# Part B of a two-part attention kernel: two projection passes split around other blocks, and the sums of the output rows moved into the next segment

## The chip, the cores and the metric

One core of a Trainium2 chip runs the whole program. The metric is the device time of one execution in microseconds (us). The engines are TensorE (PE, with its weight loads PEld), VectorE (DVE), ScalarE (ACT), GpSimd (POOL), and SyncE (SP), which here only issues DMAs.

## What is computed

The program has two parts, with their outputs side by side. Part A, a local dilated attention over 2048 rows, is not touched. Part B is a recurrence over 64 segments of 32 rows. Each segment puts 8 memory rows ahead of its 32 rows, attends over all 40 with 32 heads of 192, and the first 8 rows of its result are the memory of the next segment:

```
mem = mem0
for s in range(n_seg):                               # 64
    h = concatenate([mem, x[32*s : 32*s + 32]])      # 40 x 640
    q, k, v = h @ Wq, h @ Wk, h @ Wv                 # 32 heads x 192
    p = softmax(mask(q @ k.T * scale))
    o = (p @ v) @ Wo                                 # 40 x 640
    mem = o[:8];  outs.append(o[8:])
```

## The kernel before

**The split of the rows.** Of the 40 rows of a segment, 32 depend on the memory of the segment or stand right behind it: 8 memory rows and 24 rows of the input. They are `HX[:, 0]`, called `main`. The last 8 rows of a segment depend on no memory, so they can be projected segments ahead: `HX[:, 1]`, called `ahead`, holds them for four segments. What is projected from `ahead` is called late: the kernel keeps late queries and keys in buffers (`Lb`) and late values in the value tiles (`Vg`), and writes late output rows at the very end.

**Groups.** The 32 heads make 4 groups of 8. A segment takes the groups in the order 0, 1, 2, 3 when s is even and 3, 2, 1, 0 when s is odd. In a name such as `k.2` the number is the place in that order, not the group. Per group there are these steps, each a function of `part_b`:

- `q`, `k`, `v`: projection passes on PE (L554), 20 matmuls of 32 x 384 for `main`, five pieces (`dc`) of 4 matmuls. Where the group is renewed (`RENEW`, L295), `ahead` is projected in the same pass: 40 matmuls. One key group is renewed per segment: at s mod 4 = 0 or 3 it is the first one (`k.0`), at 1 or 2 the third (`k.2`).
- `e`: ACT (one of four by DVE) copies the projection out of PSUM (L560 for the late part, L593); `T`: DVE turns it 32 x 32 in place (L564), POOL copies the late columns (L579, L584, L600).
- `S`: 16 score matmuls (L623); `sb`, `mx`, `sub`, `send`: the softmax on DVE (L629 to L655) with the exponential on ACT (L641); the result is the tile `P`.
- `tp`: PE turns `P` (L663); `PT`: ACT or DVE spreads it (L670, L673); `mix`: PE multiplies with the values (L685); `ot`: DVE and ACT copy the result to the tile `OT` (L693), POOL copies its late rows to `OL` (L694) and sends them to HBM (L695).
- `out`: 24 matmuls with the output weights into the sum `Y` (L710); the fourth group's are the step `last`.

Between segments stand four more. `ql` projects the late rows for one query group (20 matmuls), `eql` copies them out and `Tql` turns them; DVE does it in the tile `sb`, which has one buffer, and POOL then copies four pieces of it (L584). `vl` projects them for one value group (20 matmuls), `vel` copies that out (ACT, L614, two copies). `close` makes the new memory rows of `Y`: DVE turns two halves (L522) and adds them into `HX` (L721), from where `q.0` of the next segment reads. Then it sums the output rows: ACT copies two halves of `Y` to scratch in `OT` (L725), DVE adds them to the others in `YS` (L727), and four stores of `YS` are put on a list that SP issues at `k.0` of the next segment (L765).

**What sets the order.** PE, DVE, ACT and SP run their instructions in the order in which they are written, and that is the string `ORDER` (L303; `FIRST` for segment 0). POOL's order is found by the tile framework.

**Weights.** Groups 0 and 3 share their slots for q, v and o. When the first group in a segment has been used, SP loads the other one into the slot from a copy in HBM (`change`, L412): query weights behind `q.0`, value weights behind `v.0`, output weights in two pieces behind the two halves of the first `out`. The last output group reads the latter. One fifth of a key group is swapped behind `k.0` (L399). A DMA issue of SP stands behind all earlier ones of SP.

Of the kernel before, what the change touches and what calls it, by code (L numbers as in the profile page):

```python
# [23 lines left out]
def part_a(ctx, tc, A_x, A_wqkv, A_wo, out, ident, emit_loads):  # L24
# [288 lines left out]
SHARED = (0, 3)  # L313
# [11 lines left out]
def part_b(ctx, tc, B_x, B_mem0, B_Wq, B_Wk, B_Wv, B_Wo, out, ident, n_seg, pre, mid):  # L325
    nc = tc.nc
    Dm, H, Dh, M, SEG, L = 640, 32, 192, 8, 32, 40
# [386 lines left out]
    def close(s, Y):  # L714
        if s + 1 < n_seg:
            T = [KT[:].rearrange("p f n -> p (f n)"), QT[:]]
            T = [t[:, 0:320].bitcast(FP32).rearrange("p (k n) -> p k n", n=SEG) for t in T]
            for b in range(2):
                turn32(T[b], Y[:, 160 * b:160 * b + 160])
            for b in range(2):  # L720
                nc.vector.tensor_tensor(HX[64 * b:64 * b + 64, 0, :, 0:M], T[b][0:64, :, 0:M], T[b][64:128, :, 0:M],  # L721
                                        op=ALU.add)
        half = OT[:].rearrange("p c n -> p (c n)")[:, 0:320].bitcast(FP32)
        for b in range(2):
            S_(half[64 * b:64 * b + 64], Y[64:128, 160 * b:160 * b + 160])  # L725
        for b in range(2):
            nc.vector.tensor_tensor(YS[64 * b:64 * b + 64], Y[0:64, 160 * b:160 * b + 160],  # L727
                                    half[64 * b:64 * b + 64], op=ALU.add)
        stores.extend((out2[SEG * s:SEG * s + SEG - M, Dm + 160 * j:Dm + 160 * j + 160], YS[32 * j + M:32 * j + SEG])
                      for j in range(4))  # L730
        if s + 1 == n_seg:
            while stores:
                nc.gpsimd.dma_start(*stores.pop(0))

    stores = []

    def segment(s):
        last = s + 1 == n_seg
        engine = {"S": S_, "V": V_}
        got = {}  # L740
# [10 lines left out]
        def step(name, *at):  # L751
            n = int(at[0][-1]) if at else None
            g = turn[n] if at else None
            if name in "qkv":
                project(name, g)
                if name == "q" and n == 0:
                    change(name, g, slice(0, 2))
                    change(name, g, slice(2, 5))
                    load_x(s + 1)
                if name == "v" and n == 0:  # L760
                    change(name, g)
                if name == "k" and n == 0:
                    replace(*(PAIR if g == PAIR[0][1] else PAIR[::-1]))
                    while stores:
                        nc.sync.dma_start(*stores.pop(0))  # L765
                if s == 0 and n == 0 and name != "q":
                    load_all("o", 1 if name == "k" else 2)
                if last and name == "v" and n == 1:
                    load_outputs()
            elif name == "e":  # L770
                m = at[0][0]
                got["sb", m, g] = evacuate(m, got.pop((m, g)), [engine[c] for c in EVACUATE[at[0]]])
            elif name == "T":
                m = at[0][0]
                keep = fill_late(s, m, g, got.pop(("sb", m, g)))
                turn_in_place(columns_of(m, 0, 32))
                if at[0] == "k0" and s and keep:
                    got["keep"] = keep
                elif keep:
                    keep()  # L780
                if at[0] == "k1" and "keep" in got:
                    got.pop("keep")()
            elif name == "S":
                got["S", g] = scores(g)
            elif name == "sb":
                got["t", g] = soft_begin(got.pop(("S", g)))
            elif name == "mx":
                got["mx", g] = soft_max(got["t", g])
            elif name == "sub":
                soft_exp(got["t", g], got.pop(("mx", g)))  # L790
            elif name == "send":
                soft_end(s, g, got.pop(("t", g)))
            elif name == "tp":
                got["p", g] = turn_p(g)
            elif name == "PT":
                got["PT", g] = spread_p(got.pop(("p", g)), SPREAD[n])
            elif name == "ve":
                keep_values(g, got.pop(("v", g)))
            elif name == "mix":
                got["mix", g] = mix(g, got.pop(("PT", g)))  # L800
            elif name == "ot":
                keep_mix(s, g, got.pop(("mix", g)), [engine[c] for c in HEADS[n]])
            elif name == "out":
                half = int(at[1])
                if "Y" not in got:
                    got["Y"] = ps_y.tile([128, 320], FP32, tag="y", name="Y")
                n = int(at[0])
                g = turn[n]
                project_out(got["Y"], g, range(4 * half, 4 + 2 * half), n == 0, False)
                if n == 0 and not last:  # L810
                    change("o", g, slice(4 * half, 4 + 2 * half))
                if n == 0 and half and last:
                    load_late(range(4))
# [80 lines left out]
    with tc.manual_schedule(engines={mybir.EngineType.PE, mybir.EngineType.DVE, mybir.EngineType.Activation,  # L894
                                     mybir.EngineType.SP}):
        for s in range(n_seg):
            segment(s)
        project_late()


# [67 lines left out]
```

## Time and profile before

| what | value |
|---|---|
| runs | 1717.2, 1717.04, 1709.44 us (median 1717.04) |
| the profiled execution | 1717.32 us |
| its span, first to last instruction | 1715.4 us |
| mean granted TensorE clock | 0.997 |
| busy: PE, PEld, DVE, ACT, POOL | 93%, 59%, 66%, 58%, 31% |
| moved by DMA | 474.80 MB, 277 GB/s in the mean |

A row of the timeline has start and length in us, engine, line, operation, tiles written and read, shape, count of instructions merged, and in brackets the idle time of the engine before it with what ended it. Lengths of matmuls overlap, since they are pipelined: the time that a block takes is the difference between its start and the next block's. A row of the waits has waiting engine and line, what ended the wait, us in total, times, and the longest. DMA issues stand as SPq and their time is that of the issue, not of the transfer.

### The profile page before, as it was taken

To read this page: it belongs to the slowest core of one execution; us is meant where nothing else is said; L and a number is where in the kernel's file an instruction comes from. 1 tells how busy PE (TensorE), PEld (TensorE's weight loads), DVE (VectorE), ACT (ScalarE), POOL (GpSimd) and SP (SyncE) were. 2 spreads that over 40 slices of the span, in tenths; PEclk is the share of its full clock that TensorE was granted. 3 is DMA by queue.
4 is the path that set the end of the run, shared out by engine and by line. 5 is a ranking of instruction groups with operands and counts; after the bars stand their busy time and mean duration, and the time that the engine had idled before them with its cause. 6 is when DMAs were issued, how large, how long until landed. Compare 5 with 4: busy or idle time off the path is not lost.

```text
span 1715.4 us, 82589 instructions
## 1 busy us (share of the span) xinstructions
PE 1596.4 (93%) x35702; PEld 1015.7 (59%) x35702; DVE 1130.4 (66%) x3334; ACT 989.1 (58%) x2544; POOL 536.1 (31%) x1592
## 2 busy tenths in 40 slices
PE   7999899999999999999999999899999999999988
PEld 5666555555555555555565555555555555555668
DVE  4987566667666666766666766666767666666730
ACT  3554556666665666655666665566666655665630
POOL 0201233333333333333333333333333333333320
PEclk9999999999999999999999999999999999999999
DMA  7995877778777778877777887777788777777870
GB/s 215 343 293 216 338 279 272 277 287 305 284 278 272 264 274 304 301 263 272 265 287 289 304 301 262 264 277 277 296 304 302 276 274 277 271 296 286 305 301 18
DMA packets 123816, 474.80 MB, mean 277 GB/s; under 512 B 46884, under 2 KB 61842, under 8 KB 99004
## 3 DMA queue, kind: packets, MB, share of 16 engines
q1 hardware_dynamic: 112940, 458.35, 72.0%
q0 software_dynamic: 9696, 10.30, 1.9%
q8 instruction: 280, 4.59, 1.0%
q10 hardware_dynamic: 816, 0.88, 0.2%
q14 instruction: 84, 0.69, 0.1%
HBM read 455.29 MB, written 26.78 MB: 281 GB/s over the span
## 4 chain that ended last, share of the span: by engine, by line
PE 62%; DVE 14%; DMA 13%; ACT 4%; issue 4%; POOL 3%; SPq 0%; ACTq 0%; DVEq 0%; POOLq 0%
PE acc L554 27%; PE Y L710 11%; DMA wres_o<-wcopy_o 7%; PE px L623 7%; PE pq L102 4%; PE px L685 3%; DVE sb L564 3%; PE px L663 3%; DMA wres_q<-wcopy_q 2%; POOL Lb L584 2%; ACT Vg L614 2%; ACT sb L560 2%; DVE KT L564 2%; PE px L863 2%; PE po L168 1%
## 5 line engine op out<-in xcount | busy, mean ns | idle before, releaser
L554 PEld LDWEIGHTS <-HX 128*32 128x32 bf16 x19380 | 495.9, 97 | 297.0 <-DVE HX L721 43.6
L554 PE MATMUL acc<-wres_q,HX 128*32 128x384 bf16 x6460 | 324.2, 327 | 23.0 <-DVE HX L721 19.9
L554 PE MATMUL acc<-wres_v,HX 128*32 128x384 bf16 x6460 | 325.8, 328 | 7.3 <-issue 6.5
L554 PE MATMUL acc<-wres_k,HX 128*32 128x384 bf16 x6460 | 313.8, 326 | 3.3 <-issue 2.1
L710 PE MATMUL Y<-wres_o,OT 128*32 128x320 bf16 x6120 | 278.1, 301 | 26.5 <-issue 11.6
L608 ACT CAST Vg<-acc 64x384 bf16<-64x384 f32 x512 | 241.4, 471 | 50.2 <-PE acc L554 46.4
L694 POOL COPY OL<-OT 128x96 bf16<-128x96 bf16 x256 | 158.1, 617 | 333.5 <-DMA late_o<-OL 143.9
L710 PEld LDWEIGHTS <-OT 128*32 128x32 bf16 x6144 | 148.7, 96 | 97.6 <-issue 36.3
L593 ACT CAST QT<-acc 128x384 bf16<-128x384 f32 x256 | 122.9, 480 | 102.9 <-PE px L623 96.5
L623 PE MATMUL px<-KT,QT 64*64 64x40 bf16 (+1 forms) x4096 | 138.5, 189 | 27.2 <-DVE KT L564 12.5
L695 POOL DMA_DIRECT2D late_o<-OL x256 | 137.9, 539 | 75.4 <-POOL OL L694 54.6
L600 POOL COPY QT<-Lb 128x96 bf16<-128x96 bf16 x252 | 67.6, 268 | 298.0 <-PE px L623 298.0
L623 PEld LDWEIGHTS <-QT 64*64 64x64 bf16 (+1 forms) x4096 | 107.8, 109 | 87.6 <-issue 36.2
L693 DVE CAST OT<-px 128x240 bf16<-128x240 f32 x192 | 78.2, 407 | 107.4 <-PE acc_mix L685 92.0
L670 ACT ACTIVATE PT<-px,own 128x160 bf16<-128x160 f32 x384 | 130.5, 392 | 27.5 <-PE px L663 21.5
L564 DVE STREAM_TRANSPOSE KT<-KT 128x384 bf16<-128x384 bf16 x256 | 141.5, 553 | 2.6 <-ACT KT L593 2.6
L564 DVE STREAM_TRANSPOSE QT<-QT 128x384 bf16<-128x384 bf16 x256 | 143.2, 559 | 0.0
L584 POOL COPY Lb<-sb 128x96 bf16<-128x96 bf16 x453 | 104.3, 268 | 120.9 <-DVE sb L564 120.9
L629 DVE SCALAR_TENSOR_TENSOR px<-px,mask 128x160 f32<-128x160 f32 x256 | 84.7, 331 | 85.7 <-PE px L623 82.1
L693 ACT CAST OT<-acc_mix 128x240 bf16<-128x240 f32 x256 | 92.2, 360 | 78.8 <-PE acc_mix L685 58.4
L593 ACT CAST KT<-acc 128x384 bf16<-128x384 f32 x256 | 123.2, 481 | 14.7 <-PE acc L554 6.9
L685 PEld LDWEIGHTS <-Vg 128*128 128x128 bf16 (+1 forms) x2048 | 86.5, 104 | 72.9 <-issue 25.4
(103 smaller groups left out, 1977.7 us busy)
## 6 DMA issues: line engine op xcount, KB each, us to landing
wres_v<-wcopy_v SPq DMA_DIRECT2D x64, 1920.0 KB
wres_o<-wcopy_o SPq DMA_DIRECT2D x63, 1280.0 KB
wres_q<-wcopy_q SPq DMA_DIRECT2D x64, 1152.0 KB
wres_q<-wcopy_q SPq DMA_DIRECT2D x64, 768.0 KB
wres_o<-wcopy_o SPq DMA_DIRECT2D x63, 640.0 KB
wres_k<-wcopy_k SPq DMA_DIRECT2D x64, 384.0 KB
wres_k<-in_B_Wk_dram SPq DMA_DIRECT2D x19, 384.0 KB
late_o<-OL POOLq DMA_DIRECT2D x256, 24.0 KB, 4.3
```

Source lines behind the costliest of these rows:

```text
L554: nc.tensor.matmul(ps[n][t:t + 32].rearrange("p (f n) -> p f n", n=32), lhsT=X[:, dc, :], rhs=columns(w, (m, g, dc), j), start=(dc == 0), ...
L564: nc.vector.transpose(t, t)
L584: nc.gpsimd.tensor_copy(late[m, g, t][:], rows(t))
L593: copies[1](columns_of(m, 0, 32), ps[-1][:].rearrange("p (f n) -> p f n", n=32))
L608: S_(VG[g][64 * r:64 * r + 64, r], ps[-1][64 * r:64 * r + 64])
L623: nc.tensor.matmul(Sps[64 * h:64 * h + 64, a, :], lhsT=QT[k0:k1, L * f:L * f + 64], rhs=KT[k0:k1, f, :], start=(outer == 0 and a == 0), st ...
L670: nc.scalar.activation(PT[:, :, b], pt.rearrange("p r (h n) -> p (r h) n", h=2)[:, :, 0:L], ACTF.Copy, scale=own[:, b:b + 1])
L685: nc.tensor.matmul(ps[r][lo:hi, 2 * L * k:2 * L * k + 2 * L], lhsT=VG[g][:, r, col:col + hi - lo], rhs=PT[:, 2 * r + h].rearrange("p b n - ...
L693: copy(OT[:, 6 * r:6 * r + 6].rearrange("p c n -> p (c n)"), ps[r][:, 0:6 * L])
L694: nc.gpsimd.tensor_copy(OL[:, g % 2].rearrange("p n c -> p c n"), OT[:, :, 32:L])
L695: nc.gpsimd.dma_start(late_o[s // 4][:, g, s % 4], OL[:, g % 2].rearrange("p n c -> p (n c)"))
L710: nc.tensor.matmul(Y[t:t + 32].rearrange("p (b c) -> p b c", b=2), lhsT=OT[:, slot(c), 0:32], rhs=quarter(w, u, 2 * r + gv), start=first a ...
```

## The change

Three edits of the order of steps, none of the work.

1. `vl` becomes `vl1` and `vl2`. `vl1` has two of the five pieces (8 matmuls) and stands where `vl` stood, ahead of `last`; `vl2` has the other three (12 matmuls) and stands behind `last`. Both add into the same PSUM tile.
2. The sums of the output rows leave `close` and become the step `ys`, in `keep_rows`. It stands in the next segment behind `T.q0`. The four stores are then issued by SP at that place, behind the issues of `k.0` as before. Behind the last segment `keep_rows` is called on its own, with its stores on POOL as before.
3. `q.2` becomes `qa.2` (two pieces, 8 matmuls) ahead of `S.1` and `qb.2` (three pieces, 12 matmuls) behind it.

```diff
 ORDER = """
-    q.0 e.q0 k.0 T.q0 e.k0 T.k0 q.1 k.1 S.0 sb.0 mx.0 e.q1 T.q1 v.0 e.k1 k.2 sub.0 ve.0 T.k1 S.1 send.0 q.2 v.1
+    q.0 e.q0 k.0 T.q0 ys e.k0 T.k0 q.1 k.1 S.0 sb.0 mx.0 e.q1 T.q1 v.0 e.k1 k.2 sub.0 ve.0 T.k1 qa.2 S.1 send.0 qb.2 v.1
     e.k2 sb.1 tp.0 mx.1 q.3 sub.1 e.q2 T.k2 send.1 PT.0 tp.1 T.q2 mix.0 ve.1 ot.0 S.2 sb.2 e.q3 mx.2 PT.1
     out.0.0 k.3 v.2 out.0.1 mix.1 sub.2 T.q3 e.k3 send.2 ve.2 T.k3 S.3 tp.2 ot.1 out.1.0 sb.3 out.1.1 mx.3 PT.2
-    mix.2 sub.3 v.3 send.3 tp.3 ot.2 tx ve.3 PT.3 out.2.0 out.2.1 mix.3 vl ot.3 last ql close vel eql Tql
+    mix.2 sub.3 v.3 send.3 tp.3 ot.2 tx ve.3 PT.3 out.2.0 out.2.1 mix.3 vl1 ot.3 last vl2 ql close vel eql Tql
 """
+VL_SPLIT = 2
+Q_SPLIT = 2
...
+
+    def keep_rows(s, Y):
         half = OT[:].rearrange("p c n -> p (c n)")[:, 0:320].bitcast(FP32)
         for b in range(2):
             S_(half[64 * b:64 * b + 64], Y[64:128, 160 * b:160 * b + 160])
         for b in range(2):
             nc.vector.tensor_tensor(YS[64 * b:64 * b + 64], Y[0:64, 160 * b:160 * b + 160],
                                     half[64 * b:64 * b + 64], op=ALU.add)
-        stores.extend((out2[SEG * s:SEG * s + SEG - M, Dm + 160 * j:Dm + 160 * j + 160], YS[32 * j + M:32 * j + SEG])
-                      for j in range(4))
-        if s + 1 == n_seg:
-            while stores:
-                nc.gpsimd.dma_start(*stores.pop(0))
-
-    stores = []
+        for j in range(4):
+            (nc.gpsimd if s + 1 == n_seg else nc.sync).dma_start(
+                out2[SEG * s:SEG * s + SEG - M, Dm + 160 * j:Dm + 160 * j + 160], YS[32 * j + M:32 * j + SEG])
...
+            elif name in ("qa", "qb"):
+                part = slice(0, Q_SPLIT) if name == "qa" else slice(Q_SPLIT, 5)
+                got["q", g] = project32([main], "q", g, part, got.get(("q", g)))
...
-            elif name == "vl":
-                got["vl"] = None if last else project32([ahead], "v", next_values, at=(2,))
+            elif name in ("vl", "vl1", "vl2"):
+                part = slice(VL_SPLIT if name == "vl2" else 0, VL_SPLIT if name == "vl1" else 5)
+                if not last:
+                    got["vl"] = project32([ahead], "v", next_values, part, got.get("vl"), at=(2,))
...
             elif name == "close":
                 close(s, got["Y"])
+                sums[s] = got["Y"]
+            elif name == "ys":
+                keep_rows(s - 1, sums.pop(s - 1))
```

ACT's queue at a segment's end, before: the copy for `ot.3`, then `close` (L725), `vel` (L614), `eql` (L560), and of the next segment the copies of `q.0` (L593) and of the renewed `k.0` (L560, L593).

```order
L693 CAST OT<-acc_mix 128x240
L725 COPY OT<-Y 64x160 x2
L614 CAST Vg_2997<-acc_5227 64x384 x2
L560 CAST sb<-acc_5276 128x384
L593 CAST QT<-acc_5314 128x12x32
L560 CAST sb<-acc_5339 128x384
L593 CAST KT<-acc_5340 128x12x32
```

The same place now (lines of the changed kernel are 2 to 4 higher):

```order
L695 CAST OT<-acc_mix 128x240
L616 CAST Vg_2997<-acc_5227 64x384 x2
L562 CAST sb<-acc_5276 128x384
L595 CAST QT<-acc_5310 128x12x32
L729 COPY OT<-Y 64x160 x2
L562 CAST sb<-acc_5335 128x384
L595 CAST KT<-acc_5336 128x12x32
```

The two copies of `Y` have moved from the first place behind the `OT` copy to behind the copy of `q.0`; on DVE the two sums move likewise, from behind the memory rows to between the turns of `q.0` and `k.0`.

PE's queue where the last output group begins, before: the end of `vl` (piece 4 of a value group), then `Y`.

```order
L554 LDWEIGHTS HX
L554 MATMUL acc_5227<-wres_v_4_2918,HX 32x384
L710 LDWEIGHTS OT
L710 MATMUL Y<-wres_o_0_2919,OT 32x320
L710 LDWEIGHTS OT
```

And now: `Y` begins behind piece 1.

```order
L556 LDWEIGHTS HX
L556 MATMUL acc_5227<-wres_v_1_2915,HX 32x384
L712 LDWEIGHTS OT
L712 MATMUL Y<-wres_o_0_2919,OT 32x320
L712 LDWEIGHTS OT
```

Pieces 2 to 4 follow behind the 24 matmuls into `Y`, ahead of `ql`.

PE's queue at the second scores, before: the end of `k.2`, then the score matmuls.

```order
L554 MATMUL acc_5482<-wres_k_4_81,HX 32x384
L623 LDWEIGHTS QT
L623 MATMUL px<-KT,QT 64x40
L623 LDWEIGHTS QT
L623 MATMUL px<-KT,QT 64x40
```

And now: `k.2` is followed by the first pieces of `q.2`.

```order
L556 MATMUL acc_5482<-wres_k_4_81,HX 32x384
L556 LDWEIGHTS HX
L556 MATMUL acc_5512<-wres_q_0_72,HX 32x384
L556 LDWEIGHTS HX
L556 MATMUL acc_5512<-wres_q_0_72,HX 32x384
```

Eight matmuls of the query pass have moved ahead of the 16 of the scores. SP's issues stand in the same order as before; on POOL, in segments with s mod 4 = 1 or 2, the copy of late rows to `OL` for `ot.0` has come ahead of one copy of late query columns.

More of the change, by code (lines that the diff above doesn't have):

```diff
@@ L728, in close @@
                                     half[64 * b:64 * b + 64], op=ALU.add)
-        stores.extend((out2[SEG * s:SEG * s + SEG - M, Dm + 160 * j:Dm + 160 * j + 160], YS[32 * j + M:32 * j + SEG])
-                      for j in range(4))
-        if s + 1 == n_seg:
-            while stores:
-                nc.gpsimd.dma_start(*stores.pop(0))
-    stores = []
+        for j in range(4):
+            (nc.gpsimd if s + 1 == n_seg else nc.sync).dma_start(
+                out2[SEG * s:SEG * s + SEG - M, Dm + 160 * j:Dm + 160 * j + 160], YS[32 * j + M:32 * j + SEG])
+    sums = {}
     def segment(s):
@@ L763, in step @@
                     replace(*(PAIR if g == PAIR[0][1] else PAIR[::-1]))
-                    while stores:
-                        nc.sync.dma_start(*stores.pop(0))
                 if s == 0 and n == 0 and name != "q":
@@ L897, in part_b @@
             segment(s)
+        keep_rows(n_seg - 1, sums.pop(n_seg - 1))
         project_late()
```

## The prediction

> **What bounds the kernel now.** First the page's head and its chain, to see which engine the end hangs on; then the waits, to see for whom that engine waits; then the timeline of two segments.
>
> ```profile
> span 1715.4 us, 82589 instructions
> ...
> PE 62%; DVE 14%; DMA 13%; ACT 4%; issue 4%; POOL 3%; SPq 0%; ACTq 0%; DVEq 0%; POOLq 0%
> ```
>
> The profiled execution took 1717.32 us, 1.9 over its span, and stands 0.3 above the median of the runs (1717.04). I reckon against 1717.3. TensorE (PE) carries 62% of the chain, and the rest is what it waits for.
>
> ```profile
> PE acc L554 <- DVE HX L721: 19.9, 59, 0.4
> PE px L623 <- DVE KT L564: 12.5, 35, 1.1
> PE Y L710 <- DMA wres_o<-wcopy_o: 11.1, 17, 1.7
> PE px L623 <- POOL Lb L584: 10.9, 31, 0.4
> ACT OT L725 <- POOL OL L694: 22.6, 10, 2.9
> ```
>
> Columns: total us, times, longest. The counts tell where: 59 is nearly once per segment (query 0 waits for the new memory rows), 35 and 31 are about half of the 63 segments in ORDER (scores wait for keys), 17 are waits for output weights. So a segment is a chain from the memory rows to the next memory rows, with PE full in between.
>
> Segments are of two kinds. In kind B (s mod 4 = 3 or 0; 31 of them) the first key group is renewed, so k.0 is 40 matmuls and k.2 is 20; in kind A (1 or 2; 32 of them) k.0 is 20 and k.2 is 40. A segment of kind B, with the end of the one before it:
>
> ```profile
> 802.08 1.00 PE L554 MATMUL acc<-wres_v,HX 128*32 128x384 bf16 x20
> ...
> 802.23 0.41 DVE L693 CAST OT<-px 128x240 bf16<-128x240 f32 x1 [0.74 <-PE acc_mix L685]
> ...
> 802.90 0.99 PE L710 MATMUL Y<-wres_o,OT 128*32 128x320 bf16 x24
> ...
> 803.72 0.99 PE L554 MATMUL acc<-wres_q,HX 128*32 128x384 bf16 x20
> ...
> 804.64 0.59 ACT L725 COPY OT<-Y 64x160 f32<-64x160 f32 x2 [2.03 <-DVE QT L522]
> ...
> 805.04 1.00 PE L554 MATMUL acc<-wres_q,HX 128*32 128x384 bf16 x20 [0.34 <-DVE HX L721]
> 805.13 0.96 ACT L614 CAST Vg<-acc 64x384 bf16<-64x384 f32 x2
> ...
> 805.87 1.92 PE L554 MATMUL acc<-wres_k,HX 128*32 128x384 bf16 x40
> 805.99 0.47 ACT L560 CAST sb<-acc 128x384 bf16<-128x384 f32 x1
> ...
> 807.14 0.90 POOL L584 COPY Lb<-sb 128x96 bf16<-128x96 bf16 x4 [2.86 <-DVE sb L564]
> ...
> 808.07 0.48 ACT L560 CAST sb<-acc 128x384 bf16<-128x384 f32 x1 [1.23 <-POOL Lb L584]
> ...
> 809.76 0.54 PE L623 MATMUL px<-KT,QT 64*64 64x40 bf16 x16 [0.35 <-POOL Lb L584]
> ...
> 811.05 0.99 PE L554 MATMUL acc<-wres_k,HX 128*32 128x384 bf16 x20
> ...
> 811.65 0.56 DVE L564 STREAM_TRANSPOSE KT<-KT 128x384 bf16<-128x384 bf16 x1
> ...
> 812.36 0.54 PE L623 MATMUL px<-KT,QT 64*64 64x40 bf16 x16 [0.32 <-DVE KT L564]
> ...
> 815.02 0.39 DVE L655 TENSOR_TENSOR P<-px,sm 128x128 bf16<-128x128 f32 x2
> ...
> 815.71 0.29 PE L663 MATMUL px<-ident,P 128*128 128x128 bf16 x2
> ```
>
> In order on PE: late values (vl), the last output group, late query (ql), q.0 after a wait, k.0, the first scores at 809.76 after a wait, k.2, the second scores at 812.36 after a wait, the turn of P.1 at 815.71. A block's length I take from start to start (the ends are modelled): 20 projection matmuls take 0.82 (802.08 to 802.90), so 8 take 0.33 and 12 take 0.49. Kind A:
>
> ```profile
> 756.97 0.99 PE L554 MATMUL acc<-wres_q,HX 128*32 128x384 bf16 x20
> ...
> 758.51 0.67 DVE L727 TENSOR_TENSOR YS<-Y,OT 64x160 bf16<-64x160 f32 x2 [0.27 <-ACT OT L725]
> ...
> 759.61 0.48 ACT L593 CAST QT<-acc 128x384 bf16<-128x384 f32 x1
> ...
> 760.99 1.68 SPq L765 DMA_DIRECT2D out_dram<-YS  x4
> ...
> 761.66 0.54 PE L623 MATMUL px<-KT,QT 64*64 64x40 bf16 x16
> ...
> 762.95 1.80 PE L554 MATMUL acc<-wres_k,HX 128*32 128x384 bf16 x40
> 763.16 0.35 SPq L412 DMA_DIRECT2D wres_v<-wcopy_v  x1
> ...
> 764.67 0.54 PE L623 MATMUL px<-KT,QT 64*64 64x40 bf16 x16
> 764.85 0.48 ACT L560 CAST sb<-acc 128x384 bf16<-128x384 f32 x1
> ...
> 767.77 0.39 DVE L655 TENSOR_TENSOR P<-px,sm 128x128 bf16<-128x128 f32 x2
> ...
> 768.22 0.11 PEld L663 LDWEIGHTS <-P 128*128 128x128 bf16 x2 [0.51 <-DVE P L655]
> ...
> 769.66 0.62 POOL L694 COPY OL<-OT 128x96 bf16<-128x96 bf16 x1
> ...
> 772.43 0.54 PE L623 MATMUL px<-KT,QT 64*64 64x40 bf16 x16
> ```
>
> Here neither scores row has an idle bracket: PE is the later one at 761.66 and 764.67. But the turn of P.1 starts 0.06 after P.1 ends (767.77 + 0.39 = 768.16, then 768.22): PE waits there for the softmax that began at 764.67, 3.55 earlier.
>
> **The change, part by part.** *Values' pass split, 62 boundaries.* Before the output group only 8 matmuls stand, 0.33 in place of 0.82. It can then start when its input is copied: 802.23 + 0.41, and 0.06 to pass it on as at P.1, is 802.70 in place of 802.90. Behind it stand 12 + 20 matmuls, 0.49 + 0.82 = 1.31, just the 1.32 from 803.72 to 805.04 that the memory rows need. So the wait before q.0 goes, a wait of 0.29 appears before the output group, and the gain is 0.20, not the 0.34 of the bracket: 62 × 0.20 = **-12.4**. It needs DVE and ACT to finish the copies no later than now, and they are not touched.
>
> *Rows' sums out of the close, kind B.* The ACT queue goes straight to the late values: vl ends 0.49 after ql's old start, its copies start at about 0.7, and 0.86 later (805.13 to 805.99) comes the late query's copy, at 1.6 in place of 2.27. The four POOL copies that end at 808.04, 4.32 after ql's start, end 0.7 earlier, at 3.6, so the key copy of 808.07 no longer waits for them but for k.0 itself: k.0 starts at 2.15 (805.87) and a 40-matmul pass hands its first copy over after 1.90 (762.95 to 764.85), so 4.05 in place of 4.35. From there to the scores it is 1.69 as now. First scores 0.30 earlier, 31 times: **-9.3**. The bounds are 0 (POOL is late for another reason) and 0.35, the whole bracket.
>
> *Rows' sums behind the query's turn, kind A.* ACT copies q.0 about 0.27 earlier than now (759.61 is 2.64 after ql's start; now 2.37, since q.0 follows its pass at once), then does the two L725 (0.59) and is free at 3.45. DVE's two L727 take 0.67, from 3.48 to 4.15, ahead of group 0's key turn, and from that turn's start to the scores it takes 0.71 (811.65 to 812.36): 4.12 + 0.71 = 4.83, against 4.69 now (761.66 - 756.97). So +0.15, 32 times: **+4.8**. No trace shows this order, so the bounds are wide: 0, if the turn hides the sums (no gain: they only come ahead of it), and 0.59 + 0.67 = 1.26, if both stand on the chain whole. I take the small value, since the rows add up to it. In kind B the sums are done at 4.15, before the renewed key's copy is at 4.5: hidden, with 0.4 to spare.
>
> *Query's pass split, kind B.* The second scores wait for the key's turn, 2.60 after the first scores; k.2 at 1.29 plus 0.82 plus 8 matmuls is 2.44, so they stay in place and 0.33 of PE work moves into the wait. P.1 is ready at 815.41 + 0.06 = 815.47, against 815.71 now: the gain stops at 0.24, 31 × 0.24 = **-7.4**; bounds 0 and 0.33.
>
> *The same split, kind A.* There is no wait to fill, so the second scores start 0.33 later, and behind them DVE works for 3.55 in a fixed order until P.1, for which PE already waits. Queued behind that wait on PE: the turn, mix 0, the third scores. So the loss is whole: 32 × 0.33 = **+10.6**; bounds 0 (something else sets P.1) and 0.33.
>
> *Queues passed.* SP keeps its order; the stores wait for the sums at 4.15 in place of 760.99 (4.02), 0.2 later, and their 1.68 then end at 762.9, before the values' load at 763.16. If that cover is gone, the load starts later by what is missing, 0.2 at most as these rows stand. In kind A one POOL copy for group 3's query moves behind the OL copy of 0.62 at 769.66; its reader is at 772.43, so nothing. The blocked L725 (10 times, 22.6 in all against the usual 2.03 each) may return 2 us; I leave it out of the sum and in the range.
>
> Sum: -12.4 - 9.3 + 4.8 - 7.4 + 10.6 = **-13.7**.
>
> *What is late next: the output weights.* They are loaded into a slot that the first output group has just left, and the last group reads them.
>
> ```profile
> GB/s 1 21 0 188 382 452 437 341 488 389 444 418 223 179 305 427 358 363 112 27 14 21 37 193 392 439 437 354 421 410 444 431 184 200 366 436 322 377 45 45
> ...
> q1 hardware_dynamic: 2304, 12.73, 71.3%
> ...
> 826.28 0.99 PE L710 MATMUL Y<-wres_o,OT 128*32 128x320 bf16 x24
> ```
>
> These are two segments (803 to 850) in slices of 1.18: the stream runs from slice 4 to slice 19, to about 825.3, an us before the last group at 826.28. In 17 of 62 segments it is late already. There the boundary's 0.20 is not gained, 17 × 0.20 = 3.4, and a few more become late; I take **+4.7** (bounds 0, and 12.4, the whole boundary). Forecast: 1717.3 - 13.7 + 4.7 = **1708**.
>
> The Trainium skill, page "DMA: Bandwidth & Descriptors", section "Where 436 GB/s comes from", says that about 358 GB/s per core is what HBM allows. An estimate by it: 6.4 MB per segment take 17.8 us, so from 806.9 the weights would be in at 824.7, early even after the change, and the sum would stay at -13.7. Slices of 437 to 488 here lie above that figure, and 17 late loads say that the arrival is not even, so the trace does not bear it out.
>
> **Rivals.** (1) *The weight stream takes more back.* If its end stays put while PE comes earlier, kind B loses half of 0.54 besides: 31 × 0.27 = 8.4, and the time is 1716. For it: DMA is 13% of the chain. Against: the load is issued when PE leaves the slot, so it moves along. (2) *The weights come evenly and are never late again.* No give-back: 1703.6. Against it are the 17 waits; the page's rule above is this case. (3) *Kind A does not lose at the second scores*, because P.1 hangs on the key's transposes of k.2 and not on the scores: 1708 - 10.6 = 1697. Against: DVE's order puts the scores' steps first. (4) *The sums hold the first scores.* Place: kind A, L727 ahead of the key's turn; each 0.1 us later than 4.15 costs 3.2. At 0.28 more the gain is gone; with 0.5 more it is 1724, and at the full 1.26 it is 1743. For it: the slack there is nil by my rows. Against: the rows add up to 0.15 only. (5) *The second scores in kind B move too*, so that the split does not do what it is for: 1708 + 7.4 = 1715.
>
> **How the numbers follow.** Forecast 0.50, rival 1 0.17, 2 0.09, 3 0.08, 4 0.11, 5 0.05. A measurement tells 0.5% from no change, 8.6 us: faster is below 1708.5, slower above 1725.6. The forecast lies at the edge: 0.29 of its 0.50 below it, with rivals 2 and 3 that is 0.46. Slower is the worse half of rival 4 and a little of 1: 0.08. The rest, 0.46, is within. The range 1697 to 1721 takes in rivals 1, 2, 3, 5 and the mild part of 4, and leaves its worse part and the far ends of the bounds out, which would have to fall together.
>
> **What would show it.** The boundary: the wait of q.0 for L721 falls from 19.9 to near 0, and the output group waits for its copied input; from output group to output group's end 0.20 less. Kind B: scores at 5.7 after ql's start, not 6.04, and no wait for POOL; the wait for KT gone. Kind A: 3.55 from second scores to the turn of P.1 as before, the turn 0.33 later. Weights: more than 17 waits. I am wrong if kind A's first scores come after 4.9, or if the weights' waits exceed some 16 us in all.

## The result

The changed kernel took 1690.67 us in the median of four runs (1687.39 to 1698.96), the kernel before 1716.62 beside it (1709.44 to 1717.2). The ratio is 0.9874, with a 95% interval of 0.984 to 0.9907: **faster by 1.3%**. A later comparison, six runs against eleven, gave 0.9876 [0.9845, 0.9907]. The forecast was 1708, with a range that ended at 1697: the sign was right and the gain too small.

### The profile after

The profiled execution took 1692.0 us. Its page, the span and the chain that ended last:

```profile
span 1690.1 us, 82587 instructions
...
PE 59%; DMA 19%; DVE 8%; issue 2%; ACT 2%; POOL 1%; DVEq 0%; SPq 0%; POOLq 0%
```

The span is 25.3 us shorter. VectorE's share of the chain fell from 14 to 8%, and the DMAs' rose from 13 to 19%: what waited for engines now waits more for transfers. (The lines of the code moved by 2 to 4: L554 is now L556, L560 L562, L623 L625, L663 L665, L693 L695, L710 L712, L721 L723, L725 L729, L727 L731.)

The waits of the changed kernel (waiting engine and line, what ended the wait, us in total, times, longest):

```profile
PEld L712 <- DVE OT L695: 38.5, 62, 1.8
...
PE Y L712 <- DMA wres_o<-wcopy_o: 14.7, 20, 2.2
...
PEld L556 <- DVE HX L723: 13.9, 59, 0.5
...
ACT sb L562 <- POOL QT L602: 12.8, 31, 0.4
...
PE px L665 <- DVE P L657: 11.5, 28, 0.5
PEld L625 <- POOL Lb L586: 11.2, 31, 0.4
...
PE px L625 <- DVE KT L566: 1.6, 2, 1.1
```

Against the rows of before: the matmuls' own wait of `q.0` for the memory rows (19.9, 59) is gone; what is left, 13.9, is that of the weight loads, which run beside matmuls. The second scores' wait for the key (12.5, 35) is down to 1.6. The wait of the last output group for its copied input, 5.4 us in 10 times before, now comes nearly once per boundary (38.5, 62), and the turn of `P.1` waits 28 times: kind A. The waits for output weights are 20 for 17. In the timelines, 16 of the 20 (13 of the 17 before) stand not at the start of the last group but ahead of its 17th matmul, the first one that reads the second, smaller load.

One boundary into a segment of kind A, from the timeline of the changed kernel:

```profile
764.59 0.51 PE L556 MATMUL acc<-wres_v,HX 128*32 128x384 bf16 x8
...
765.19 0.66 PEld L712 LDWEIGHTS <-OT 128*32 128x32 bf16 x24 [0.48 <-DVE OT L695]
...
766.02 0.66 PE L556 MATMUL acc<-wres_v,HX 128*32 128x384 bf16 x12
766.51 1.83 PE L556 MATMUL acc<-wres_q,HX 128*32 128x384 bf16 x40
...
768.17 0.99 PE L556 MATMUL acc<-wres_k,HX 128*32 128x384 bf16 x20
...
770.84 0.54 PE L625 MATMUL px<-KT,QT 64*64 64x40 bf16 x16
...
773.75 0.39 DVE L657 TENSOR_TENSOR P<-px,sm 128x128 bf16<-128x128 f32 x2
773.76 0.50 PE L556 MATMUL acc<-wres_q,HX 128*32 128x384 bf16 x8
...
774.19 0.54 PE L625 MATMUL px<-KT,QT 64*64 64x40 bf16 x16
...
777.73 0.29 PE L665 MATMUL px<-ident,P 128*128 128x128 bf16 x2 [0.45 <-DVE P L657]
```

Eight late-value matmuls, the wait for `OT`, the output group, the other twelve, and late query and `q.0` as one block of 40 with no wait between. From the late values to `k.0` it is 768.17 - 764.59 = 3.58, against 805.87 - 802.08 = 3.79 before. The first scores come 770.84 - 766.02 = 4.82 after the start of `vl2`, which is where `ql` stood (forecast 4.83). From the second scores to the turn of `P.1` it is 777.73 - 774.19 = 3.54 (3.55 before), so the 0.33 by which the scores are late stays.

A segment of kind B:

```profile
809.80 0.51 PE L556 MATMUL acc<-wres_v,HX 128*32 128x384 bf16 x8
...
810.40 0.12 PEld L712 LDWEIGHTS <-OT 128*32 128x32 bf16 x8 [0.49 <-DVE OT L695]
...
811.02 0.73 PE L712 MATMUL Y<-wres_o,OT 128*32 128x320 bf16 x16 [0.16 <-issue]
...
811.57 0.66 PE L556 MATMUL acc<-wres_v,HX 128*32 128x384 bf16 x12
...
813.71 1.80 PE L556 MATMUL acc<-wres_k,HX 128*32 128x384 bf16 x40
...
815.14 0.28 POOL L602 COPY QT<-Lb 128x96 bf16<-128x96 bf16 x1
815.34 0.99 PE L556 MATMUL acc<-wres_q,HX 128*32 128x384 bf16 x20
815.45 0.48 ACT L562 CAST sb<-acc 128x384 bf16<-128x384 f32 x1 [0.41 <-POOL QT L602]
...
817.14 0.54 PE L625 MATMUL px<-KT,QT 64*64 64x40 bf16 x16
```

The key copy of L562 starts 815.45 - 813.71 = 1.74 after its pass, and the scores 817.14 - 811.57 = 5.57 after `vl2`'s start: 6.04 before, 5.74 forecast. The output group lasts 811.57 - 810.40 = 1.17 here and 766.02 - 765.19 = 0.83 above: the difference is a hole in front of its later pieces. Of such holes more below.

Over all segments, medians of the distances between the starts of PE's blocks in the two timelines (us per segment; 32 of kind A, 28 to 30 of kind B, where every mark is in the trace):

| stretch | A before | A after | B before | B after | forecast A, B |
|---|---|---|---|---|---|
| `k.0` to first scores | 2.54 | 2.67 | 3.89 | 3.42 | +0.15, -0.30 |
| first to second scores | 3.02 | 3.34 | 2.59 | 2.59 | +0.33, 0 |
| second scores to turn of `P.1` | 3.55 | 3.54 | 3.36 | 3.11 | 0, -0.24 |
| `mix.3` to the last output group | 1.26 | 1.05 | 1.26 | 1.05 | -0.20 for the boundary |

Every step moved as forecast, but for kind B's first scores: 0.47 in place of 0.30.

### The profile page after: what moved, and what is told of

The parts are those of the page before. It is cut to its first block, busy times and chain, and to the rows that moved or that the text cites. A ratio compares the mean times of both kernels' runs of the same rounds, so it can differ in the third digit from the quotient of the medians.

```text
span 1690.1 us, 82587 instructions
## 1 busy us (share of the span) xinstructions
PE 1598.0 (95%) x35702; PEld 1011.6 (60%) x35702; DVE 1142.1 (68%) x3334; ACT 1000.2 (59%) x2544; POOL 538.4 (32%) x1592
## 4 chain that ended last, share of the span: by engine, by line
PE 59%; DMA 19%; DVE 8%; issue 2%; ACT 2%; POOL 1%; DVEq 0%; SPq 0%; POOLq 0%
PE acc L556 34%; DMA wres_o<-wcopy_o 10%; PE Y L712 10%; PE px L625 6%; DMA late_o<-OL 4%; DMA wres_q<-wcopy_q 3%; PE px L687 2%; PE px L665 2%; DVE KT L566 2%; PE px L871 2%; PE acc L871 1%; DVE OT L695 1%; PE acc_mix L687 1%; ACT OT L729 1%; DVE sb L566 1%
## 5 line engine op out<-in xcount | busy, mean ns | idle before, releaser
L556 PEld LDWEIGHTS <-HX 128*32 128x32 bf16 x19380 | 492.6, 97 | 267.3 <-issue 21.8
L556 PE MATMUL acc<-wres_v,HX 128*32 128x384 bf16 x6460 | 337.6, 328 | 5.0 <-issue 3.5
L556 PE MATMUL acc<-wres_q,HX 128*32 128x384 bf16 x6460 | 327.9, 330 | 5.4 <-DMA wres_q<-wcopy_q 4.4
L556 PE MATMUL acc<-wres_k,HX 128*32 128x384 bf16 x6460 | 308.4, 326 | 1.2 <-issue 1.2
L712 PE MATMUL Y<-wres_o,OT 128*32 128x320 bf16 x6120 | 276.4, 302 | 34.6 <-DMA wres_o<-wcopy_o 14.7
L610 ACT CAST Vg<-acc 64x384 bf16<-64x384 f32 x512 | 242.5, 474 | 50.0 <-PE acc L556 46.1
L712 PEld LDWEIGHTS <-OT 128*32 128x32 bf16 x6144 | 142.3, 96 | 119.0 <-DVE OT L695 38.5
L602 POOL COPY QT<-Lb 128x96 bf16<-128x96 bf16 x252 | 75.2, 299 | 280.6 <-PE px L625 280.6
L625 PEld LDWEIGHTS <-QT 64*64 64x64 bf16 (+1 forms) x4096 | 112.1, 108 | 69.3 <-issue 38.7
L625 PE MATMUL px<-KT,QT 64*64 64x40 bf16 (+1 forms) x4096 | 139.4, 188 | 9.2 <-issue 1.9
L695 DVE CAST OT<-px 128x240 bf16<-128x240 f32 x192 | 78.3, 408 | 97.3 <-PE acc_mix L687 71.7
L695 ACT CAST OT<-acc_mix 128x240 bf16<-128x240 f32 x256 | 92.3, 360 | 86.1 <-PE acc_mix L687 59.9
L616 ACT CAST Vg<-acc 64x384 bf16<-64x384 f32 x134 | 63.5, 474 | 128.9 <-PE acc L556 128.0
```

The source lines that it names most:

```text
L556: nc.tensor.matmul(ps[n][t:t + 32].rearrange("p (f n) -> p f n", n=32), lhsT=X[:, dc, :], rhs=columns(w, (m, g, dc), j), start=(dc == 0), ...
L610: S_(VG[g][64 * r:64 * r + 64, r], ps[-1][64 * r:64 * r + 64])
L625: nc.tensor.matmul(Sps[64 * h:64 * h + 64, a, :], lhsT=QT[k0:k1, L * f:L * f + 64], rhs=KT[k0:k1, f, :], start=(outer == 0 and a == 0), st ...
L695: copy(OT[:, 6 * r:6 * r + 6].rearrange("p c n -> p (c n)"), ps[r][:, 0:6 * L])
L712: nc.tensor.matmul(Y[t:t + 32].rearrange("p (b c) -> p b c", b=2), lhsT=OT[:, slot(c), 0:32], rhs=quarter(w, u, 2 * r + gv), start=first a ...
```

## Experiments

Two questions stood: is each edit worth what the steps say, and why did the time fall by more than their forecast sum.

### One edit at a time

The values' pass split alone, on the kernel before:

```diff
-    ... out.2.1 mix.3 vl ot.3 last ql close vel eql Tql
+    ... out.2.1 mix.3 vl1 ot.3 last vl2 ql close vel eql Tql
```

> Edit 1 alone: the values' pass split around the last output group, the rest as before. Theory by terms (each edit gives what its own place shows in the trace): output group 0.20 us earlier at each of 62 boundaries, of which the late output weights take some 0.04 back, so 10 us less than before, ratio 0.994; in the profile the four blocks from the values' pass to the end of query 0 take 3.58 us in place of 3.78. Rival (the weights take it back, as the prediction reckoned): 4.7 of 12.4 given back or more, 8 us less or nothing, ratio 0.9955 to 1.000, with more than 17 waits of the output group for its weights.

Measured: 1708.13 against 1717.84, ratio 0.9956 [0.9931, 0.9981], so -7.6 us [-11.9, -3.3]. Its waits:

```profile
PEld L710 <- DVE OT L693: 39.0, 63, 2.3
...
PE acc L554 <- DVE HX L721: 0.3, 1, 0.3
```

The exchange of waits is whole: 19.9 to 0.3 before `q.0`, and the new one before the output group. The -12.4 of the steps lies just outside the interval: some of it is lost, about as much as the rival had (8 us less). The sign that the rival named did not come, though: the group waits for its weights 16 times, not more than 17. The time alone does not part the two.

The rows' sums moved alone (the changed kernel with both splits taken back):

```diff
-    ... T.k1 qa.2 S.1 send.0 qb.2 v.1
+    ... T.k1 S.1 send.0 q.2 v.1
-    ... mix.3 vl1 ot.3 last vl2 ql close vel eql Tql
+    ... mix.3 vl ot.3 last ql close vel eql Tql
```

> Edit 2 alone: the rows' sums moved into the next segment, both passes whole. Theory by terms: in kind B (31 segments) the first scores 0.47 us earlier, since the renewed key's copy starts 1.74 after its pass starts, in kind A (32) 0.13 later: 31 x 0.47 - 32 x 0.13 = 10 us less, ratio 0.994. Rival (the terms of the prediction, a copy 1.90 after the pass starts): 31 x 0.30 - 32 x 0.15 = 4.5 less, ratio 0.9975.

Measured: 1707.07 against 1717.84, ratio 0.9938 [0.9912, 0.9965], so -10.6 [-15.1, -6.0]. One of the ten executions, the profiled one, took 4996 us and is not in the ratio, so the same kernel was run once more for its profile.

> The rows' sums moved alone, once more for its profile. Both theories: about 1707 as timed; the medians of its steps should show kind B's first scores 0.36 earlier (keys of group 1 to first scores at 0.99 for 1.35) and kind A's 0.13 later, and no change elsewhere.

1709.61 in one run beside 1715.85. The medians are as expected: `k.1` to first scores 0.99 for 1.35 in kind B (and 0.10 more from `k.0` to `q.1`), 1.05 for 0.92 in kind A. That is -0.46 x 31 + 0.13 x 32 = -10, just the time measured. The forecast had -9.3 + 4.8 = -4.5 for this edit, which lies outside the interval: here is the mis-sized term. The waits show that the rest of the chain stayed as it was:

```profile
PE acc L556 <- DVE HX L723: 19.6, 59, 0.4
...
PE px L625 <- DVE KT L566: 11.9, 35, 1.1
PEld L625 <- POOL Lb L586: 11.2, 31, 0.4
```

The query's pass split alone, on the kernel before:

```diff
-    ... T.k1 S.1 send.0 q.2 v.1
+    ... T.k1 qa.2 S.1 send.0 qb.2 v.1
```

> Edit 3 alone: the second query pass split around the second scores, the rest as before. Theory by terms: kind A loses 0.33 at the turn of P.1, kind B gains 0.24: 32 x 0.33 - 31 x 0.24 = 3 us more than before, ratio 1.002. Rival (kind A does not lose, P.1 hangs on something else than the second scores): 7 us less, ratio 0.9957.

Measured: 1712.94 against 1717.84, ratio 0.9985 [0.9953, 1.0016], so -2.6 [-8.1, +2.7]: the rival's -7 lies just inside the interval and the theory's +3 (1.002) just outside, so the time settles nothing here. Its waits show both sides of the trade:

```profile
PE px L663 <- DVE P L655: 10.4, 26, 0.5
...
PE px L623 <- DVE KT L564: 1.6, 2, 1.1
```

The wait of kind B is filled (12.5 to 1.6), and in kind A a wait of 10.4 is opened behind the second scores. The three edits add up to -20.8; together they made -21.6 (0.9874). No interplay shows, with 4 to 5 us of uncertainty on each.

### Kind A's loss, and the stream of weights

If kind A's 0.33 is real, leaving the split out there should save 10 us. The changed kernel with this in the loop over the order:

```diff
+        if s % 4 in (1, 2):
+            order = order.replace("qa.2 S.1 send.0 qb.2", "S.1 send.0 q.2")
```

> The changed kernel, but with the query pass split in kind B alone; in kind A (s mod 4 = 1 or 2) it stands whole behind the second scores as before. Theory by terms: 32 x 0.33 = 10.6 us less than the changed kernel, about 1680, ratio to before 0.978. Rival (kind A does not lose): as the changed kernel, about 1691, ratio 0.985.

Measured: 1690.46, ratio 0.9855 [0.9814, 0.9895]; the changed kernel had 0.9874. The theory fell: in the medians of its steps kind A is shorter by 0.39 (21.80 for 22.19), its mean is 22.61 for 22.71. Something takes the saving back. The loads that renew the weights run beside every segment, so three kernels were run with hardly any:

```diff
-        nc.sync.dma_start(res[new], copied[new])
+        end = 64 if new[0] == "k" else unit_cols(new)
+        nc.sync.dma_start(res[new][:, 0:end], copied[new][:, 0:end])
-        nc.sync.dma_start(slots[m, other][:, a:a + n * len(olds)], copied[m, other][:, a:a + n * len(olds)])
+        nc.sync.dma_start(slots[m, other][:, a:a + 64], copied[m, other][:, a:a + 64])
```

The kernel before:

> The kernel before, with the loads that renew the weights of the queries, values, output and keys cut to 64 columns each, so that nearly nothing streams in behind the segments (the outputs are computed with weights that are partly not the reference's). Two theories of where the slack of a segment goes, the part by which the mean of a segment lies above its median (0.90 and 0.76 us in the kernel before, 52 us in all). Theory W: the stream of weights sets a floor to the segments, which takes up what the engines save in kind A; without it the waits for weights go (15 us by the stalls counted in the trace of before) and the differences between versions become those of the medians of their steps. Then this runs at about 1702, ratio 0.991. Rival F: the slack is made by TensorE's holes in front of instructions that nothing releases (34 us in the trace of before), in whatever version; then the time falls by the 15 us all the same, but the versions keep the distances they had with the stream.

The changed kernel:

> The changed kernel with the same loads cut to 64 columns (part of the weights is then not the reference's). Theory W: against the kernel before with the same cut, only the medians of the steps count: kind A +0.40 x 32 = +13, kind B -1.00 x 31 = -31, start and end -4, so 22 less than that, about 1680 (0.979). Rival F: the distance of the full kernels, 26, and the waits for weights of its own trace (23) away: about 1668 (0.972).

The changed kernel with the query's pass whole in kind A:

> The changed kernel with group 2's query pass whole in kind A, and the same loads cut to 64 columns (part of the weights is then not the reference's). With the full loads the split in kind A cost nothing that the time shows (1690.46 without it, 1690.67 with it), though the medians of the steps differ by 0.39 x 32 = 12. Theory W: without the stream this difference comes out, 12 less than the run before it, ratio about 0.972. Rival F: it does not come out, within 3 of the run before it.

Measured: 1653.81 (1651.66 to 1654.98), 1632.39 (1631.96 to 1635.04) and 1622.65 (1622.42 to 1623.37); ratios to the kernel before 0.9636 [0.9576, 0.9697], 0.9517 [0.9467, 0.9567], 0.9457 [0.9408, 0.9507]. The first two levels are some 48 us lower than theory W had them: it counted only the waits that end with a landing weight, and much else went with the stream, the holes of "issue" among it. The distances answer the question: 21.4 from the first to the second (W expected 22, F 26), 9.7 from the second to the third (W 12, F under 3). **On the distances theory W holds**: without the stream, kind A's loss is there, as forecast.

Groups of PE in the two kernels with the loads cut, kernel before and changed kernel (busy, mean ns, idle time in front and what ended it):

```profile
L555 PE MATMUL acc<-wres_q,HX 128*32 128x384 bf16 x6460 | 320.2, 327 | 21.4 <-DVE HX L722 21.4
...
L711 PE MATMUL Y<-wres_o,OT 128*32 128x320 bf16 x6120 | 265.3, 300 | 0.2
```

```profile
L557 PE MATMUL acc<-wres_q,HX 128*32 128x384 bf16 x6460 | 321.2, 327 | 0.3 <-DVE HX L724 0.3
...
L713 PE MATMUL Y<-wres_o,OT 128*32 128x320 bf16 x6120 | 266.3, 301 | 7.5 <-issue 0.8 <-DVE OT L696 0.5
```

With the loads whole, the output group's idle time is 26.5 before (11.6 of it "issue", 11.1 weights) and this after:

```profile
L712 PE MATMUL Y<-wres_o,OT 128*32 128x320 bf16 x6120 | 276.4, 302 | 34.6 <-DMA wres_o<-wcopy_o 14.7 <-DVE OT L695 9.9 <-issue 3.6
```

To see whether the saving shows at all with the stream, three kernels were timed side by side: the changed one,

> The changed kernel once more, beside the two that follow, to set the distances among the three. Both theories: ratio 0.987, about 1691.

the one with kind A's pass whole,

> Group 2's query pass whole in kind A, once more. Without the stream of weights this saves 9.7 us (1632.39 to 1622.65). Theory W, the stream takes the saving back: within 4 of the run before it. Rival E, the saving is there in full and the first comparison (1690.46 beside 1690.67, four runs each) was scatter: 10 less than the run before it, about 1681 (0.981).

and the same with the sums further back in kind A:

```diff
+            order = order.replace("qa.2 S.1 send.0 qb.2", "S.1 send.0 q.2").replace("ys e.k0 T.k0", "e.k0 T.k0 ys")
```

> As the run before it, and in kind A the rows' sums stand behind the transposes of group 0's keys (T.k0) and not ahead of their evacuation, which should give the first scores of kind A their 0.13 x 32 = 4 us back by the medians. Theory W: nothing of it is seen, within 4 of the changed kernel. Rival E: 14 less than the changed kernel, about 1677.

Measured: 1695.41, ratio 0.9876 [0.9845, 0.9907]; 1691.85, 0.9867 [0.9831, 0.9903]; 1687.11, 0.9838 [0.9806, 0.987]. The kernel with the pass whole is faster by 0.2 and 3.6 us in the medians of the two comparisons, by 3.3 and 1.5 by their ratios, not by 9.7, and rival E's 0.981 lies outside the interval: theory W again, within the scatter. The last is the fastest kernel of the study that computes everything; at 0.4% below the changed one, with overlapping intervals, neither "within 4" nor 14 is what it did, and it settles nothing.

### Which part of the stream

Only the output weights' loads cut, in the changed kernel:

```diff
+        end = a + (64 if m == "o" else n * len(olds))
-        nc.sync.dma_start(slots[m, other][:, a:a + n * len(olds)], copied[m, other][:, a:a + n * len(olds)])
+        nc.sync.dma_start(slots[m, other][:, a:end], copied[m, other][:, a:end])
```

> The changed kernel with the loads of the output weights alone cut to 64 columns (a part of these weights is then not the reference's); the loads of queries, values and keys are whole. The cut of all of them took 58 us (1690.67 to 1632.39), though the waits that end with a landing weight were 23 us in the trace. Theory H: most of the 58 us are waits for a landing weight and holes ahead of instructions that nothing releases, which come from the traffic as such; with the output weights gone the 17 us of waits for them go, the traffic falls by about a quarter, and the holes mostly stay: about 1665 to 1675. Rival O: the whole cost hangs on the output weights, which are the last of each round to land: about 1635 to 1645.

Measured: 1648.11 (1646.98 to 1649.92), 0.9607 [0.9575, 0.9639]. Of the 63 us between 1695.41 and 1632.39 (61 by the ratios), 47 went with the output weights: 3 above rival O's range and 17 below theory H's, which is out. A window of 1000 us in the middle (length, busy time of PE, PEld, DVE, ACT and POOL, granted clock, share of DMA busy, GB/s), changed kernel, then with the output weights cut, then with all cut:

```profile
400.00:1400.00 1000.00, 953.90 (x22036) 587.50 (x22028) 698.97 (x2204) 628.06 (x1629) 355.87 (x1059) 1.00 0.77 288
```

```profile
400.00:1400.00 1000.00, 975.59 (x22732) 600.00 (x22720) 721.92 (x2278) 648.61 (x1686) 366.54 (x1091) 1.00 0.56 211
```

```profile
400.00:1400.00 1000.00, 979.70 (x22940) 603.96 (x22936) 726.78 (x2292) 652.01 (x1698) 370.05 (x1103) 1.00 0.08 16
```

The output weights' quarter of the traffic (288 to 211 GB/s) costs 47 us, the other 195 GB/s 16. But the waits for landed output weights in the trace of the changed kernel were only 14.7 us. One other thing went with them: GpSimd's copy into `OL` waits for the store of an earlier `OL`, 149.6 us in the changed kernel, 3.6 here. Three buffers in place of two tell whether that is the way. They need room, so first a control in which `YS` lies in the tile `XS`:

```diff
-    YS = xpool.tile([128, 160], BF16, name="YS")
+    YS = XS
```

> A control for the two runs that follow, which need room: the changed kernel with the rows' sums YS in the tile of the input rows XS, whose load is then issued behind that of the values and not behind that of the queries. The load comes 15 us ahead of its reader still, so all theories: within 4 of the changed kernel, ratio about 0.987.

```diff
-    OL = cpool.tile([128, 2, M, 12], BF16, name="OL")
+    OL = cpool.tile([128, 3, M, 12], BF16, name="OL")
```

> The control with three buffers in place of two for the late rows on their way to HBM (OL). In the trace of the changed kernel GpSimd's copy into OL waits 99 times, 149.6 us in all, until an earlier store has landed (7.8 without the stream of weights, 3.6 with the output weights' loads cut), and 20 times the copies into OT behind it wait for GpSimd, 22.7 us on VectorE. Theory L: that is a second way by which the stream costs time; the 20 blocked copies go, and with them most of TensorE's 10.5 us of waits for OT: 8 to 12 less than the control, about 1682 (0.980). Rival N: the output weights arrive when they arrive, and what is not waited for OT is waited for them: within 4 of the control.

The same with kind A's pass whole and the sums further back:

> As the run before it, with group 2's query pass whole in kind A and the rows' sums behind T.k0 there, which save 14 by the medians and 5 in the runs so far. Theory L, with the further claim that the blocked OT is where the saving was lost: 10 to 14 less than the run before it, about 1670. Rival N: 5 less than the run before it or nothing.

Measured: 1699.89, 0.9915 [0.9885, 0.9945] for the control, 4 to 7 us above the changed kernel, which no theory expected (the intervals overlap; its waits for output weights are 21.6 us where the changed kernel has 14.7, and why is open); 1698.45, 0.9897 [0.9863, 0.993] with three buffers, within 4 of the control as rival N had it; 1694.69, 0.9874 [0.9843, 0.9905] with both, 4 less again, rival N once more. The waits of the control:

```profile
POOL OL L696 <- DMA late_o<-OL: 147.4, 98, 3.9
...
PE Y L712 <- DMA wres_o<-wcopy_o: 21.6, 30, 1.8
...
PE Y L712 <- DVE OT L695: 12.6, 16, 1.9
```

and with three buffers:

```profile
PE Y L712 <- DMA wres_o<-wcopy_o: 29.0, 40, 1.6
...
POOL OL L696 <- DMA late_o<-OL: 3.1, 2, 2.1
...
PE Y L712 <- DVE OT L695: 1.0, 2, 0.5
```

**Theory L fell, and the rows show how**: the stores' waits went (147.4 to 3.1) and PE's waits for `OT` with them (12.6 to 1.0), and the waits for output weights rose from 21.6 to 29.0, 30 times to 40. The time fell by 1.4 (3 by the ratios). Who comes earlier to the last output group waits there for its weights. Whether a saving in kind A goes the same way is not shown: in the second run with the pass whole those waits are longer and more than the changed kernel's 14.7, 20,

```profile
PE Y L712 <- DMA wres_o<-wcopy_o: 18.1, 26, 1.5
```

but in the first they were 15.1 us, 20 times, no more than in the changed kernel.

## Why the prediction was wrong

Counted from 1717.3 - 13.7 + 4.7, the median came out 17 us lower. 7.7 of it are sizes of engine terms (21.4 without the stream, 13.7 forecast), 4.7 the give-back, and 5 depend on which runs are compared: by the ratio the changed kernel is at 1717.04 x 0.9875 = 1695.6, and still below the range.

*Values' pass, -12.4.* Right in mechanism and size: 0.21 per boundary, the wait exchanged as drawn. Alone it gave 7.6; with the stream the gain is lost at some boundaries, as in the hole behind 810.40 above.

*Rows' sums, kind B, -9.3.* **The failed step**: "a 40-matmul pass hands its first copy over after 1.90 (762.95 to 764.85)". It is 1.74. The row at 764.85 had no idle bracket, so ACT was not waiting for PE there; its rows before show what it did:

```profile
763.87 0.96 ACT L608 CAST Vg<-acc 64x384 bf16<-64x384 f32 x2
764.85 0.48 ACT L560 CAST sb<-acc 128x384 bf16<-128x384 f32 x1
```

ACT was busy until 764.83. The distance was that of ACT's queue and not of the pass. What the pass itself takes shows where ACT stands idle for it. In the changed kernel the copy L562 starts 1.74 after the pass, with a bracket that names a copy of POOL's, L602, which ends at 815.42; PE leaves `k.0` for `q.1` at 815.34. Which of the two sets the start shows in the run with the sums moved alone:

```profile
826.06 1.80 PE L556 MATMUL acc<-wres_k,HX 128*32 128x384 bf16 x40
...
826.94 0.27 POOL L602 COPY QT<-Lb 128x96 bf16<-128x96 bf16 x1
...
827.79 0.48 ACT L562 CAST sb<-acc 128x384 bf16<-128x384 f32 x1 [0.41 <-issue]
```

Here POOL's copy has ended 0.58 before, and the copy still starts 827.79 - 826.06 = 1.73 after the pass, as in the other segments of kind B of this run: the pass sets it. So the first scores came 0.47 earlier and not 0.30, which is worth 0.17 x 31 = 5.3. The upper bound of 0.35, "the whole bracket", was no bound: the weight loads of the scores still wait for POOL (11.2, 31 times), since everything ahead of that wait moved. Some 0.1 of the 0.47 lies in `k.0` itself, which the forecast left as it was: from `k.0` to `q.1` it is 1.62 for 1.73 in the medians. The sign "no wait for POOL" failed by name, since the profile puts L562's wait of 0.41 down to POOL, but not in substance.

*Rows' sums, kind A, +4.8.* Right: +0.13 for +0.15, by the place forecast. (The sum has a slip: it starts from 4.12, where the sentence before it has the sums end at 4.15, and 4.15 + 0.71 - 4.69 would be +0.17.) Rival 4 did not come.

*Query's pass, -7.4 and +10.6.* Right in kind B (-0.25 per segment for -0.24) and in kind A: without the stream, 9.7. Rivals 3 and 5 did not come. But "So the loss is whole" is true of the engines only. In the kernel with its stream a segment of kind A has slack from the weights, and giving the 0.33 back changed the time by 0 to 4.

*What is late next, +4.7.* **The other failed step**: "There the boundary's 0.20 is not gained", with nothing set against it. The waits rose about as said (20 for 17, 14.7 us for 11.1), and still nothing net was given back: 21.4 without the stream and 21.6 with it. Against the kernels with the loads cut, the mean of a segment rises through the stream by 0.89 in kind A and 0.93 in kind B before, by 0.72 and 1.07 after (one profile each; a second one of the changed kernel has the same signs with other sizes): kind B gives back 0.14 x 31 = 4.3, and kind A, which got slower, pays 0.17 x 32 = 5.4 less. The forecast charged the stream to the steps that gain and forgot to credit it to the one that loses. Rival 1 did not come; rival 2, "the weights come evenly and are never late again", was right that nothing is given back, but not by its reason: they are late as before.

The Trainium skill, page "DMA: Bandwidth & Descriptors", section "Where 436 GB/s comes from", gives 358 GB/s per core as a limit; that a load below it lands early was the prediction's inference. The measured mean of 288 GB/s lies below the limit, and weights were still late 20 times, so the trace does not bear the inference out.

What the stream costs can be added up from PE's own rows. The profiled executions of the changed kernel with the stream and with all loads cut have spans of 1690.1 and 1629.9 us. Of the 60 between them, PE's waits make 40 (74.3 for 33.9 in all): late weights of every kind are 22.0 for none, the waits for `OT` 11.7 for 1.0, the holes 13.2 for 1.5, and the wait for `P` is 3.3 shorter. The other 21 lie in PE's busy time, 1598.0 and 1576.8 us for the same 35702 matmuls; ends of matmuls are modelled, so short stops between them can be in it. With the output weights alone cut, the waits are 43.5 and the busy time is 1584.3.

What stays open: what lengthens the busy time, and by which way the output weights bring the holes and the rest of their 47 us. Whether it is their traffic in the way of other transfers or the order in which the loads land was not separated.

## What to carry to other kernels

A distance between two rows is a property of the first only if the second shows an idle bracket; without one, look at what the second's engine was doing. The bracket names what came last by the profile, and where two come within a tenth of a us, a run in which one of them is early tells which it is. Where a transfer runs beside every round of a loop, as here, charge it to the whole round: it took back part of what early steps save, and it also hid what late steps lose. To price edits of a few tenths in such a kernel, cut the transfer's size: the runs of the kernel before then lay within some 3 us and not 21, and the distances between versions came out as the sums of their steps.

## What the runs showed of the hardware

Holes on PE in front of instructions that nothing releases ("issue") come with the DMA traffic. In the kernel before they are 11.6 us in front of the output group's matmuls, up to 1.9 long, and 9.6 in front of the projections; with the loads cut (16 GB/s for 283) neither row is there. The amount of traffic alone does not give their size: over all lines they are 28.8 us in the kernel before and 13.2 in the changed kernel, at nearly the same rate, and still 10.6 with the output weights cut (211 GB/s). The Trainium skill, page "Runtime: NRT & Kernel Launch", section "Instruction fetch mechanics", says that fetching instructions is mostly hidden behind execution. No run here shows whether these holes are instruction fetches; the runs show only that they go when the stream of weights goes.

The scatter of a kernel's runs went with the same loads: 1704.7 to 1725.85 for the kernel before in one comparison, 1651.66 to 1654.98 for it with all of them cut, on the same chip. With the output weights' loads alone cut, the changed kernel lay within 1646.98 to 1649.92, for 1688.35 to 1698.54 with them.
